# Retention, MoE and SOLU on one core: one two-bank PSUM tile for each attention unit, a fixed order of its products, and state products on 64x64 quarters

## The chip, the cores and the metric

One Trainium2 chip, one of its cores. The metric is the device time of one execution, in microseconds; of a kernel's runs the median counts. TensorE multiplies into PSUM, which has eight banks of 128 x 512 float32; VectorE and ScalarE read PSUM and write SBUF; GpSimd helps from SBUF; SyncE issues most of the DMA transfers.

## The reference

Three stages in a row. The first is a retention (linear attention with a decaying state), for 4 batches, 8 heads, 768 tokens and a head size of 64; the second a feed-forward with a piecewise activation; the third a feed-forward with a softmax-gated activation and a normalisation.

```python
gamma = 1.0 - 2.0 ** (-5.0 - np.arange(H))
for t in range(S):
    state = gamma * state + einsum('bhd,bhe->bhde', k[:, :, t], v[:, :, t])
    y[:, :, t] = scale * einsum('bhd,bhde->bhe', q[:, :, t], state)
x = y.transpose(0, 2, 1, 3).reshape(3072, 512)
...
h = x @ w_in                                   # 512 -> 2048
g = where(h >= 1, h, where(h <= -1, 0, (h + 1) ** 2 / 4))
x = g @ w_out                                  # 2048 -> 512
...
h = x @ w2_in                                  # 512 -> 1024
solu = h * softmax(h)
ln = (solu - mean) / sqrt(var + 1e-6) * g_ln
out = ln @ w2_out                              # 1024 -> 512
```

## The kernel before

**Attention.** The 768 tokens of a batch are six chunks of 128. A unit `u` is one chunk of one batch with all eight heads; there are 24, `u = 6 * batch + chunk`. Heads go in four pairs `p`; in `qk` (transposed, head size on the partitions) the first head of a pair (`o = 0`) lies on partitions 0 to 63 and the second (`o = 1`) on 64 to 127. A unit has two groups of products, all in float32, where one product becomes two matrix instructions:

- the first products, L153: `k` by `q` within the chunk, eight products, `o = 0` into PSUM tile `qp0` and `o = 1` into `qp1`, each with the 64 rows of its half of the array. VectorE multiplies each tile by a decay mask (`sm`, L162).
- the second group: queries by the state (L173, four products on the whole array; the state is block diagonal in a pair, so half of what is multiplied is zero), masked scores by values (L177, eight products, each into 64 output partitions) into `pv`, and the update of the state (L183, eight products of 64 columns) into `sp`. A unit that is first in its batch (0, 6, 12, 18) has no L173, one that is last (5, 11, 17, 23) no L183.

Then `split` (L88, L89) writes `pv` as a rounded part `xh` and a rest `xl` into the x tiles of its block, and ScalarE and VectorE scale the state and add `sp` to it (L190, L196).

**MoE.** Tokens are also cut into six blocks of 512, four units each (units 0 to 3 make block 0, and so on). A slot is one block and one of 16 slices `f` of the 2048 columns: `moe_h` does 12 products of 512 columns (L273) into `hp`, ScalarE and VectorE make `gh` and `gl` from it, and `moe_out` does 12 more (L301) into four accumulators two slots later. The order of the slots is written out in `segs`: block 0 with f 0 to 5, block 1 with f 0 to 11, block 0 with f 6 to 15, block 1 with f 12 to 15, then blocks 2 to 5 whole. The x tiles are double buffered by block, so those of block 2 take the place of block 0's. The weights arrive as 64-bit words and are converted on ScalarE and VectorE (`conv_w`), slice by slice ahead of their first use, up to some 155 us.

**SOLU.** From about 640 us on, 24 token tiles go through `h2` (L400), transposes (L441) and `outp` (L452).

**What sets the order.** The program's text gives priorities, and a planner with its own model of times puts the instructions of each engine in an order; the engines then run that order and wait where data isn't there. Attention from unit 8 on is traced with a raised priority (`HP_ATT`), so that the planner takes its instructions as soon as it thinks them ready.

**PSUM.** `ps_acc` has four banks (the accumulators, units 0 to 3, parts of SOLU), `ps_h` two, and `ps_a` two tiles of one bank each. From unit 4 on a unit's four tiles take turns in `ps_a`: `qp0`, `qp1`, `pv`, `sp`. A tile can be written when the one before it in that bank has been read.

Of the kernel before, what the change touches and what calls it, by code (L numbers as in the profile page):

```python
# [9 lines left out]
F32 = mybir.dt.float32  # L10
# [4 lines left out]
ALU = mybir.AluOpType  # L15
# [20 lines left out]
NWP = 2 * CPB  # L36
STEP0 = 7
W0 = -4
# [10 lines left out]
def kernel(  # L49
# [24 lines left out]
    ps_a = ctx.enter_context(tc.tile_pool(name="ps_a", bufs=2, space=bass.MemoryType.PSUM))  # L74
# [6 lines left out]
    gdec = const.tile([128, NPAIR, 1], F32, tag="gdec", name="gdec")  # L81
    g_sb = const.tile([128, NF2], F32, tag="g_sb", name="g_sb")

    def fl(t):
        return t.bitcast(F32)

# [42 lines left out]

    def attention(u, env):  # L130
# [4 lines left out]
        ppool, ptag = (ps_acc, "acc") if blk == 0 else (ps_a, "pa")  # L135
        early = u < NWP

# [6 lines left out]
        with (ExitStack() if early else tc.issue_after(state["last_w"].ins)):  # L144
            nc.sync.dma_start(qk, qk_t[b, c])
            nc.sync.dma_start(kv, kv_t[b, c])
        yield
        yield
        qp = [ppool.tile([128, NPAIR, C], F32, tag=ptag, name=f"qp{o}") for o in range(2)]
        for p in range(NPAIR):  # L150
            for o in range(2):
                r = slice(64 * o, 64 * o + 64)
                pe.matmul(qp[o][:, p, :], qk[r, 1, p, :], qk[r, 0, p, :], start=True, stop=True)  # L153
        if not first:
            qn = attp.tile([128, NPAIR, C], F32, tag="qn", name="qn", bufs=1)
            ve.tensor_tensor(out=qn, in0=qk[:, 0], in1=qdec, op=ALU.mult)
# [3 lines left out]
        for o in range(2):  # L160
            t = attp.tile([128, NPAIR, C], F32, tag="sm", name="sm", bufs=2)
            ve.tensor_tensor(out=t, in0=qp[o], in1=dmat[:, o], op=ALU.mult)  # L162
# [7 lines left out]
        pv = ppool.tile([128, NPAIR, C], F32, tag=ptag, name="pv")  # L170
        if not first:
            for p in range(NPAIR):
                pe.matmul(pv[:, p, :], st[:, p, :], qn[:, p, :],  # L173
                          start=(p == 0), stop=False, skip_group_check=True)
        for p in range(NPAIR):
            for o in range(2):
                pe.matmul(pv[64 * o:64 * o + 64, p, :], kv[:, 1, 2 * p + o, :], sm[o][:, p, :],  # L177
                          start=(first and p == 0), stop=(p == NPAIR - 1), skip_group_check=True)
        if not last:
            sp = ppool.tile([128, NPAIR, D], F32, tag=ptag, name="sp")  # L180
# [353 lines left out]
```

## Time and profile before

| | us |
|---|---|
| three runs | 931.03, 931.36, 934.76 |
| median | 931.36 |
| profiled execution | 931.8 |
| its span (first to last instruction) | 930.1 |
| TensorE busy in the span | 918.8 |
| VectorE, ScalarE, GpSimd busy | 579.4, 396.4, 26.3 |

The busy time of an engine is the time in which it had at least one instruction running; matrix instructions are pipelined, so their lengths overlap, and what a group costs is read from its start to the start of the next one. The rest of the profiled time lies outside the span. The TensorE clock that was granted is 1.00 in most stretches and lower in two windows of the first 17 us.

### The profile page before, as it was taken

To read this page: it belongs to the slowest core of one execution; us is meant where nothing else is said; L and a number is where in the kernel's file an instruction comes from. 1 tells how busy PE (TensorE), PEld (TensorE's weight loads), DVE (VectorE), ACT (ScalarE), POOL (GpSimd) and SP (SyncE) were. 2 spreads that over 40 slices of the span, in tenths; PEclk is the share of its full clock that TensorE was granted. 3 is DMA by queue.
4 is the path that set the end of the run, shared out by engine and by line. 5 is a ranking of instruction groups with operands and counts; after the bars stand their busy time and mean duration, and the time that the engine had idled before them with its cause. 6 is when DMAs were issued, how large, how long until landed. Compare 5 with 4: busy or idle time off the path is not lost.

```text
span 930.1 us, 12709 instructions
## 1 busy us (share of the span) xinstructions
PE 918.8 (99%) x4936; PEld 758.8 (82%) x4936; DVE 579.4 (62%) x1332; ACT 396.4 (43%) x725; POOL 26.3 (3%) x28
## 2 busy tenths in 40 slices
PE   8899999999999999999999999999999999999998
PEld 7788888887888887888888888888888888888886
DVE  5999997234444324422336238932988888888884
ACT  2668866333233333333336338842333333333322
POOL 3100100000010000000000000000000000000000
PEclk8999999999999999999999999999999999999999
DMA  9921821005342203200024004211101010100000
GB/s 344 417 111 46 314 72 46 24 1 163 122 123 69 68 23 113 69 23 1 23 85 165 1 0 159 76 64 46 45 35 69 24 69 23 69 23 24 24 24 35
DMA packets 25004, 75.08 MB, mean 81 GB/s; under 512 B 3184, under 2 KB 3312, under 8 KB 24176
## 3 DMA queue, kind: packets, MB, share of 16 engines
q1 hardware_dynamic: 23792, 72.18, 21.6%
q10 hardware_dynamic: 1152, 2.10, 0.9%
q8 instruction: 39, 0.64, 0.3%
q14 instruction: 21, 0.17, 0.1%
HBM read 59.58 MB, written 14.68 MB: 80 GB/s over the span
## 4 chain that ended last, share of the span: by engine, by line
PE 94%; DMA 4%; DVE 1%; ACT 1%; SPq 0%; issue 0%; DVEq 0%; ACTq 0%
PE acc L301 28%; PE hp L273 28%; PE h2p L400 14%; PE op L452 14%; PE qp L153 3%; PE tp L441 2%; PE pv L177 2%; PE pv L173 2%; DMA w_raw<-in_w_in_dram 1%; DMA xs<-x2p 1%; DMA kv<-in_kv_t_dram 1%; PE sp L183 1%; DMA dmat<-in_xtab_dram 0%; DVE xs L314 0%; DVE wm L111 0%
## 5 line engine op out<-in xcount | busy, mean ns | idle before, releaser
L301 PE MATMUL acc<-gh,w 128*128 128x512 f32 x768 | 198.6, 391 | 0.4 <-DVE xs L314 0.4
L273 PE MATMUL hp<-xh,w 128*128 128x512 f32 x768 | 195.1, 392 | 1.5 <-ACT w L116 0.8
L273 PEld LDWEIGHTS hp<-xh,w 128*128 128x128 f32 x768 | 143.0, 188 | 32.7 <-ACT xh L88 0.9
L301 PEld LDWEIGHTS acc<-gh,w 128*128 128x128 f32 x768 | 143.4, 188 | 31.5 <-DVE xs L314 1.0
L281 DVE SCALAR_TENSOR_TENSOR cs<-cs,hp 128x512 f32<-128x512 f32 x96 | 65.8, 685 | 149.4 <-ACT cs L280 149.0
L279 ACT ACTIVATE cs<-hp,half 128x512 f32<-128x512 f32 x96 | 66.1, 689 | 206.5 <-PE hp L273 193.1
L301 PE MATMUL acc<-gl,w 128*128 128x512 f32 x384 | 110.8, 393 | 0.0
L273 PE MATMUL hp<-xl,w 128*128 128x512 f32 x384 | 106.2, 393 | 0.0
L400 PE MATMUL h2p<-w,x2h 128*128 128x512 f32 x384 | 97.1, 395 | 0.0
L89 DVE TENSOR_TENSOR gl<-cs,gh 128x512 fp32r<-128x512 f32 x96 | 67.8, 706 | 40.5 <-ACT gh L88 40.1
L452 PE MATMUL op<-w,lh 128*128 128x512 f32 x384 | 91.4, 390 | 0.2 <-ACT lh L88 0.2
L273 PEld LDWEIGHTS hp<-xl,w 128*128 128x128 f32 x384 | 71.5, 188 | 15.9 <-issue 0.3
L452 PEld LDWEIGHTS op<-w,lh 128*128 128x128 f32 x384 | 71.9, 188 | 15.4 <-ACT lh L88 0.5
L301 PEld LDWEIGHTS acc<-gl,w 128*128 128x128 f32 x384 | 71.5, 188 | 15.6 <-issue 0.3
L88 ACT ACTIVATE gh<-cs 128x512 fp32r<-128x512 f32 x96 | 60.5, 630 | 51.1 <-DVE cs L281 50.7
L400 PEld LDWEIGHTS h2p<-w,x2h 128*128 128x128 f32 x384 | 70.5, 188 | 13.7
L280 ACT ACTIVATE cs<-cs 128x512 f32<-128x512 f32 x96 | 60.6, 631 | 2.7 <-ACT cs L279 0.2
L410 ACT ACTIVATE e<-h2p,st 128x512 f32<-128x512 f32 x48 | 32.6, 686 | 50.1 <-DVE st L427 38.3
L400 PE MATMUL h2p<-w,x2l 128*128 128x512 f32 x192 | 51.6, 390 | 0.0
L162 DVE TENSOR_TENSOR sm<-qp,dmat 128x512 f32<-128x512 f32 x48 | 31.8, 685 | 27.8 <-PE qp L153 26.4
L88 ACT ACTIVATE x2h<-x2r 128x512 fp32r<-128x512 f32 x24 | 15.1, 631 | 77.8 <-PE h2p L400 59.5
L452 PE MATMUL op<-w,ll 128*128 128x512 f32 x192 | 47.7, 390 | 0.0
(66 smaller groups left out, 1013.1 us busy)
## 6 DMA issues: line engine op xcount, KB each, us to landing
qk<-in_qk_t_dram SPq DMA_DIRECT2D x24, 512.0 KB, 4.3
kv<-in_kv_t_dram SPq DMA_DIRECT2D x24, 512.0 KB, 4.1
w_raw<-in_w_in_dram SPq DMA_DIRECT2D x24, 512.0 KB, 8.0
w_raw<-in_w_out_dram SPq DMA_DIRECT2D x24, 512.0 KB, 6.8
x2d<-xs SPq DMA_DIRECT2D x24, 256.0 KB, 2.7
x2r<-x2d SPq DMA_DIRECT2D x6, 1024.0 KB, 4.8
out_dram<-o SPq DMA_DIRECT2D x24, 256.0 KB, 2.0
x2p<-xs SPq DMA_DIRECT2D x8, 256.0 KB, 2.7
```

The lines of the kernel that those rows point to most:

```text
L88: sc.activation(hi, src, AF.Copy)
L89: ve.tensor_tensor(out=lo, in0=src, in1=fl(hi), op=ALU.subtract)
L153: pe.matmul(qp[o][:, p, :], qk[r, 1, p, :], qk[r, 0, p, :], start=True, stop=True)
L162: ve.tensor_tensor(out=t, in0=qp[o], in1=dmat[:, o], op=ALU.mult)
L273: pe.matmul(hp, l[:, k * 128:(k + 1) * 128], r[:, k, :], start=(n == 0), stop=(n == 3 * KD - 1))
L279: sc.activation(cs, hp, AF.Relu, bias=half, scale=0.5)
L280: sc.activation(cs, cs, AF.Square)
L281: ve.scalar_tensor_tensor(cs, cs, 1.0, hp, op0=ALU.min, op1=ALU.max)
L301: pe.matmul(acc[d][:, :BLK], l[:, d * 128:(d + 1) * 128], r, start=(first and m == 1), stop=(last and m == 3))
L400: pe.matmul(hps[n], l[:, k, :], w2i[k, n][part], start=(m == 0), stop=(m == 3 * KD - 1))
L410: sc.activation(e[:, n, :], hps[n], AF.Exp, bias=st[:, 2:3], accum_out=st[:, 3 + n:4 + n])
L452: pe.matmul(op, l[:, f, :], w2o[f][part], start=(n == 0), stop=(n == 3 * NF2 - 1))
```

## The change

- `ps_a` holds one tile of two banks (`pa`). From unit 4 on a unit takes it once for `qp0` and `qp1`, and writes `pv` and `sp` into the same tile afterwards; the next unit takes it when everything of this one has been read. In `h2` every other token tile uses it too.
- `in_row` ties the TensorE instructions traced inside it to the order in which they are traced, each to the one before, with an edge for the planner and no wait on the chip. From unit 4 on it holds the first products, and the second group, of a unit.
- From unit 12 on (`quad`) pairs 2 and 3 are loaded with their two heads exchanged between the partition halves (`load_swapped`: three transfers in place of one). The state of a head is kept in 64 x 64, and the product with it reads one half of the rows and writes one half of the output partitions: eight products, two for each of the four quarters. `pv` is two tiles, one a bank, by the half of the rows that was read; `sp` shares the second bank. `split` goes in four pieces of 64 partitions. Unit 12 also makes exchanged copies of the decay tables.

```diff
@@ -1,4 +1,4 @@
-from contextlib import ExitStack
+from contextlib import ExitStack, contextmanager
 import numpy as np
@@ -34,7 +34,9 @@
 SA, SB = 6, 12
 LD, CL = 7, 4
 NWP = 2 * CPB
+QUAD = 2 * NCH
 STEP0 = 7
+ROW = CPB
 W0 = -4
 WARM = 40
 PER = 4
@@ -71,7 +73,7 @@
     cv = ctx.enter_context(tc.tile_pool(name="cv", bufs=2))
     ps_acc = ctx.enter_context(tc.tile_pool(name="ps_acc", bufs=4, space=bass.MemoryType.PSUM))
     ps_h = ctx.enter_context(tc.tile_pool(name="ps_h", bufs=2, space=bass.MemoryType.PSUM))
-    ps_a = ctx.enter_context(tc.tile_pool(name="ps_a", bufs=2, space=bass.MemoryType.PSUM))
+    ps_a = ctx.enter_context(tc.tile_pool(name="ps_a", bufs=1, space=bass.MemoryType.PSUM))
     x2d = [dpool.tile([128, KD, BLK], F32, tag=f"x2d{b}", name=f"x2d{b}") for b in range(NBLK)]
     x2p = [dpool.tile([128, KD, BLK], F32, tag=f"x2p{b}", name=f"x2p{b}") for b in range(2)]
@@ -79,10 +81,24 @@
     half = const.tile([128, 1], F32, tag="half", name="half")
     vdec = const.tile([128, H, 1], F32, tag="vdec", name="vdec")
     gdec = const.tile([128, NPAIR, 1], F32, tag="gdec", name="gdec")
+    gdec2 = const.tile([128, NPAIR, 1], F32, tag="gdec2", name="gdec2")
     g_sb = const.tile([128, NF2], F32, tag="g_sb", name="g_sb")
     def fl(t):
         return t.bitcast(F32)
+    @contextmanager
+    def in_row():
+        done, last = {i.name for i in nc.cur_bb.bb.instructions}, None
+        yield
+        for i in nc.cur_bb.bb.instructions:
+            if i.name in done or i.engine != mybir.EngineType.PE:
+                continue
+            if last is not None:
+                tc.add_manual_dep(i, last.name, mybir.DependencyInfo(
+                    mybir.DependencyClass.NoSync, mybir.DependencyReason.DATA), reason="in a row")
+            last = i
     def split(src, hi, lo):
         sc.activation(hi, src, AF.Copy)
@@ -127,13 +143,34 @@
+    def load_swapped(dst, src):
+        n = NPAIR // 2
+        ax = (slice(None),) * (len(dst.shape) - 3)
+        nc.sync.dma_start(dst[(slice(None), *ax, slice(0, n))], src[(slice(None), *ax, slice(0, n))])
+        for h in range(2):
+            nc.sync.dma_start(dst[(slice(64 * h, 64 * h + 64), *ax, slice(n, 2 * n))],
+                              src[(slice(64 - 64 * h, 128 - 64 * h), *ax, slice(n, 2 * n))])
     def attention(u, env):
         b, c = divmod(u, NCH)
         first, last = c == 0, c == NCH - 1
         blk, cb = divmod(u, CPB)
         attp = env["attp"]
-        ppool, ptag = (ps_acc, "acc") if blk == 0 else (ps_a, "pa")
-        early = u < NWP
+        if blk == 0:
+            def banks(*names):
+                return [ps_acc.tile([128, 512], F32, tag="acc", name=n) for n in names]
+        else:
+            both = []
+            def banks(*names):
+                if not both:
+                    both.append(ps_a.tile([128, 2, 512], F32, tag="pa", name="pa"))
+                return [both[0][:, n] for n in range(len(names))]
+        early, quad = u < NWP, u >= QUAD
         def tile_of(name, *shape):
             if early:
@@ -142,24 +179,40 @@
         qk, kv = tile_of("qk", NPAIR, C), tile_of("kv", H, D)
         with (ExitStack() if early else tc.issue_after(state["last_w"].ins)):
-            nc.sync.dma_start(qk, qk_t[b, c])
+            if not quad:
+                nc.sync.dma_start(qk, qk_t[b, c])
+            else:
+                load_swapped(qk, qk_t[b, c])
             nc.sync.dma_start(kv, kv_t[b, c])
         yield
         yield
-        qp = [ppool.tile([128, NPAIR, C], F32, tag=ptag, name=f"qp{o}") for o in range(2)]
-        for p in range(NPAIR):
-            for o in range(2):
-                r = slice(64 * o, 64 * o + 64)
-                pe.matmul(qp[o][:, p, :], qk[r, 1, p, :], qk[r, 0, p, :], start=True, stop=True)
+        if u == QUAD:
+            env["qdec"] = cv.tile([128, NPAIR, C], F32, tag="wp", name="qdec2", bufs=2)
+            env["gdec"] = gdec2
+            with tc.issue_after(state["last_w"].ins):
+                load_swapped(env["qdec"], xtab_d)
+                load_swapped(gdec2, gdec_d)
+            gp.tensor_tensor(out=env["qdec"], in0=env["qdec"], in1=gdec2.to_broadcast([128, NPAIR, C]), op=ALU.mult)
+            env["dmat"] = [cv.tile([128, NPAIR, C], F32, tag="wm", name="dmat2", bufs=3) for _ in range(2)]
+            for r in range(2):
+                sc.activation(env["dmat"][r][:, :2], dmat[:, r, :2], AF.Copy)
+                sc.activation(env["dmat"][r][:, 2:], dmat[:, 1 - r, 2:], AF.Copy)
+        qp = [t.rearrange("a (p c) -> a p c", p=NPAIR) for t in banks("qp0", "qp1")]
+        with (in_row() if u >= ROW else ExitStack()):
+            for p in range(NPAIR):
+                for o in range(2):
+                    r = slice(64 * o, 64 * o + 64)
+                    pe.matmul(qp[o][:, p, :], qk[r, 1, p, :], qk[r, 0, p, :], start=True, stop=True)
         if not first:
             qn = attp.tile([128, NPAIR, C], F32, tag="qn", name="qn", bufs=1)
-            ve.tensor_tensor(out=qn, in0=qk[:, 0], in1=qdec, op=ALU.mult)
+            ve.tensor_tensor(out=qn, in0=qk[:, 0], in1=env["qdec"], op=ALU.mult)
         if not last:
             gp.tensor_tensor(out=kv[:, 0], in0=kv[:, 0], in1=vdec.to_broadcast([128, H, D]), op=ALU.mult)
         sm = []
         for o in range(2):
             t = attp.tile([128, NPAIR, C], F32, tag="sm", name="sm", bufs=2)
-            ve.tensor_tensor(out=t, in0=qp[o], in1=dmat[:, o], op=ALU.mult)
+            ve.tensor_tensor(out=t, in0=qp[o], in1=env["dmat"][o], op=ALU.mult)
             sm.append(t)
         yield
         if cb == 0:
@@ -167,21 +220,58 @@
                              env["xp"].tile([128, KD, BLK], F32R, tag="xl", name="xl"))
         xh, xl = env["x"][blk]
         tk = slice(cb * C, cb * C + C)
-        pv = ppool.tile([128, NPAIR, C], F32, tag=ptag, name="pv")
-        if not first:
-            for p in range(NPAIR):
-                pe.matmul(pv[:, p, :], st[:, p, :], qn[:, p, :],
-                          start=(p == 0), stop=False, skip_group_check=True)
-        for p in range(NPAIR):
-            for o in range(2):
-                pe.matmul(pv[64 * o:64 * o + 64, p, :], kv[:, 1, 2 * p + o, :], sm[o][:, p, :],
-                          start=(first and p == 0), stop=(p == NPAIR - 1), skip_group_check=True)
-        if not last:
-            sp = ppool.tile([128, NPAIR, D], F32, tag=ptag, name="sp")
+        if quad:
+            res = banks("pv0", "pv1")
+            pv = [t[:, :256].rearrange("a (j c) -> a j c", j=2) for t in res]
+            sp = res[1][:, 256:].rearrange("a (p d) -> a p d", p=NPAIR)
+            with (in_row() if u >= ROW else ExitStack()):
+                if not first:
+                    for j in range(2):
+                        for g in range(2):
+                            for r in range(2):
+                                o = r ^ g
+                                pe.matmul(pv[r][64 * o:64 * o + 64, j, :], st[64 * r:64 * r + 64, 2 * g + j, :D],
+                                          qn[64 * r:64 * r + 64, 2 * g + j, :], start=(j == 0), stop=False, skip_group_check=True)
+                for r in (1, 0):
+                    for j in range(2):
+                        for o in range(2):
+                            p = 2 * (r ^ o) + j
+                            pe.matmul(pv[r][64 * o:64 * o + 64, j, :], kv[:, 1, 2 * p + o, :], sm[r][:, p, :],
+                                      start=(first and j == 0), stop=(j == 1), skip_group_check=True)
+                if not last:
+                    for p in range(NPAIR):
+                        for r in range(2):
+                            h = 2 * p + (r ^ (p // 2))
+                            pe.matmul(sp[64 * r:64 * r + 64, p, :], kv[:, 0, h, :], kv[:, 1, h, :],
+                                      start=True, stop=True, skip_group_check=True)
+            for r in (1, 0):
+                for o in range(2):
+                    g, rows = r ^ o, slice(64 * o, 64 * o + 64)
+                    split(pv[r][rows], xh[rows, 2 * g:2 * g + 2, tk], xl[rows, 2 * g:2 * g + 2, tk])
+            if first:
+                ve.tensor_copy(st[:, :, :D], sp)
+            elif not last:
+                for p in range(NPAIR):
+                    sc.activation(st[:, p, :D], st[:, p, :D], AF.Copy, scale=gdec2[:, p, :])
+                ve.tensor_tensor(out=st[:, :, :D], in0=sp, in1=st[:, :, :D], op=ALU.add)
+            return
+        res = banks("pv", "sp")
+        pv = res[0].rearrange("a (p c) -> a p c", p=NPAIR)
+        sp = res[1][:, :NPAIR * D].rearrange("a (p d) -> a p d", p=NPAIR)
+        with (in_row() if u >= ROW else ExitStack()):
+            if not first:
+                for p in range(NPAIR):
+                    pe.matmul(pv[:, p, :], st[:, p, :], qn[:, p, :],
+                              start=(p == 0), stop=False, skip_group_check=True)
             for p in range(NPAIR):
                 for o in range(2):
-                    pe.matmul(sp[64 * o:64 * o + 64, p, :], kv[:, 0, 2 * p + o, :], kv[:, 1, 2 * p + o, :],
-                              start=True, stop=True)
+                    pe.matmul(pv[64 * o:64 * o + 64, p, :], kv[:, 1, 2 * p + o, :], sm[o][:, p, :],
+                              start=(first and p == 0), stop=(p == NPAIR - 1), skip_group_check=True)
+            if not last:
+                for p in range(NPAIR):
+                    for o in range(2):
+                        pe.matmul(sp[64 * o:64 * o + 64, p, :], kv[:, 0, 2 * p + o, :], kv[:, 1, 2 * p + o, :],
+                                  start=True, stop=True)
         split(pv, xh[:, :, tk], xl[:, :, tk])
         if last:
             return
@@ -220,7 +310,7 @@
     st = attp.tile([128, NPAIR, 128], F32, tag="state", name="state", bufs=1)
     gp.memset(st, 0.0)
-    env = {"attp": attp, "xp": xp, "x": {}}
+    env = {"attp": attp, "xp": xp, "x": {}, "qdec": qdec, "gdec": gdec, "dmat": [dmat[:, o] for o in range(2)]}
@@ -391,8 +481,11 @@
         def h2(t):
             hi, lo = x2s.pop(t)
-            pool, tag = ((ps_a, "pa"), (ps_acc, "acc"))[t % 2]
-            hps = [pool.tile([128, 512], F32, tag=tag, name="h2p") for _ in range(2)]
+            if t % 2:
+                hps = [ps_acc.tile([128, 512], F32, tag="acc", name="h2p") for _ in range(2)]
+            else:
+                pa = ps_a.tile([128, 2, 512], F32, tag="pa", name="h2p")
+                hps = [pa[:, n] for n in range(2)]
             for n in range(2):
                 m = 0
                 for (l, part) in ((hi, 0), (hi, 1), (lo, 0)):
```

## Rows read from the trace of the kernel before

**Rows 1.** Part 1 of the page: busy time, share of the span, instructions of each engine.

```profile
PE 918.8 (99%) x4936; PEld 758.8 (82%) x4936; DVE 579.4 (62%) x1332; ACT 396.4 (43%) x725; POOL 26.3 (3%) x28
```

**Rows 2.** Timeline of TensorE (start, length, group, count), unit 14 and unit 15's first products.

```profile
271.69 1.16 PE L153 MATMUL qp<-qk 64*128 64x128 f32 x16
272.78 1.43 PE L301 MATMUL acc<-gh,w 128*128 128x512 f32 x5
274.04 1.07 PE L301 MATMUL acc<-gl,w 128*128 128x512 f32 x4
274.95 1.98 PE L273 MATMUL hp<-xh,w 128*128 128x512 f32 x8
...
277.90 1.05 PE L173 MATMUL pv<-qn,state 128*128 128x128 f32 x8
278.88 1.09 PE L177 MATMUL pv<-sm,kv 128*64 128x128 f32 x16
279.81 0.63 PE L183 MATMUL sp<-kv 128*64 128x64 f32 x16
280.37 1.89 PE L301 MATMUL acc<-gh,w 128*128 128x512 f32 x7
...
285.83 1.16 PE L153 MATMUL qp<-qk 64*128 64x128 f32 x16
```

**Rows 3.** Timeline of TensorE, the first half of unit 17's first products.

```profile
312.68 1.98 PE L273 MATMUL hp<-xh,w 128*128 128x512 f32 x8
314.59 1.16 PE L153 MATMUL qp<-qk 64*128 64x128 f32 x8
315.67 1.19 PE L273 MATMUL hp<-xl,w 128*128 128x512 f32 x4
```

**Rows 4.** Timeline of TensorE, unit 18, its second group of products.

```profile
358.99 0.43 PE L177 MATMUL pv<-sm,kv 128*64 128x128 f32 x2
359.36 0.49 PE L273 MATMUL hp<-xl,w 128*128 128x512 f32 x1
359.78 0.98 PE L177 MATMUL pv<-sm,kv 128*64 128x128 f32 x13
...
361.26 0.73 PE L273 MATMUL hp<-xl,w 128*128 128x512 f32 x2
```

**Rows 5.** Windows of all engines: length, busy us of each, then granted clock, DMA.

```profile
10.00:17.00 7.00, 7.00 (x74) 6.20 (x72) 4.65 (x8) 1.87 (x5) 2.92 (x3) 0.61 1.02 390
...
40.00:77.00 37.00, 37.00 (x244) 29.86 (x244) 35.39 (x66) 23.65 (x43) 1.04 (x1) 1.00 0.35 143
...
245.00:345.00 100.00, 99.98 (x635) 81.97 (x634) 39.27 (x63) 35.41 (x65) 5.76 (x5) 1.00 0.27 85
```

**Rows 6.** Timeline of TensorE, first gap of unit 0 (in brackets: idle before).

```profile
9.78 0.48 PE L177 MATMUL pv<-sm,kv 128*64 128x128 f32 x1 [3.22 <-DVE sm L162]
```

**Rows 7.** Timeline of VectorE, the weight conversion that block 0's f=5 waits for.

```profile
72.18 0.68 DVE L117 TENSOR_TENSOR w<-wm,w 128x512 fp32r<-128x512 f32 x1
```

**Rows 8.** Timeline of TensorE, h of block 0, f=5.

```profile
74.02 2.01 PE L273 MATMUL hp<-xh,w 128*128 128x512 f32 x8
```

**Rows 9.** Timeline of ScalarE, units 8 and 9 leave PSUM.

```profile
201.74 1.09 ACT L88 ACTIVATE xh<-pv 128x512 fp32r<-128x512 f32 x2 [1.79 <-PE hp L273]
```

**Rows 10.** Timeline of TensorE, units 9, 10, 11 and the first h of block 2.

```profile
207.75 0.69 PE L183 MATMUL sp<-kv 128*64 128x64 f32 x16
208.37 1.16 PE L153 MATMUL qp<-qk 64*128 64x128 f32 x8
...
227.97 1.16 PE L153 MATMUL qp<-qk 64*128 64x128 f32 x16
...
241.74 1.07 PE L273 MATMUL hp<-xh,w 128*128 128x512 f32 x4
```

**Rows 11.** Timeline of all engines, unit 14 on VectorE and ScalarE.

```profile
273.10 1.28 DVE L162 TENSOR_TENSOR sm<-qp,dmat 128x512 f32<-128x512 f32 x2
...
281.45 0.69 DVE L89 TENSOR_TENSOR xl<-pv,xh 128x512 fp32r<-128x512 f32 x1
```

## The prediction

> **What bounds the kernel now.** I read the page's busy times first: TensorE is busy for 918.8 of 930.1 us and no other engine for more than 62% [rows 1]. So only TensorE time that goes away, or a new TensorE wait, can move the end. Next the windows: between 245 and 345 us TensorE stands for 0.02 us of 100, with VectorE and ScalarE at some 40% [rows 5]. Then the timeline of TensorE, to see what a unit of attention costs there and what it costs its neighbours. Last, two places where another engine paces the work: the start, where VectorE is full (35.39 of 37 us [rows 5]), and the step into block 2.
>
> The reader should see three things in the timeline. Sixteen first products in a row, which alternate between the two row halves, take 1.09 us (271.69 to 272.78, [rows 2]); eight of one half alone take 1.08 us too (314.59 to 315.67, [rows 3]). So the halves run side by side if they alternate, and a unit whose two banks are filled in two separate groups pays 2.17. I count eight such units among the twenty from unit 4 on: 5, 6, 9, 10, 12, 17, 21 and 22. Second, a group costs its neighbours something: eight MoE products take 1.91 us before it instead of 1.81, five take 1.26 behind it instead of 1.13 (at 0.227 each, from 274.04 to 274.95) [rows 2, 3]. That is 0.10 in and 0.13 out. Third, in units 6, 10, 12, 18 and 22 the second group is torn apart, as the second `sm` comes after the first product.
>
> **The change, part by part.** The sum is made against the profiled execution's 931.8 us, 0.4 above the median of 931.36; it carries over to the median unchanged.
>
> One tile and a fixed order for the first products. The two banks come free together, so the planner has no reason to start one half early: 8 x 1.09 = 8.7 us saved [rows 3]. Each of these units also loses one cut, 0.2 x 8 = 1.6.
>
> The fixed order of the second group. Torn, `pv` and `sp` take 0.37 + 1.48 = 1.85 us and the single MoE product between them 0.42 instead of 0.23 [rows 4]; whole they take 0.93 + 0.56 = 1.49 [rows 2]. That is 0.55 a unit. Unit 6 starts with `pv` and may still be torn; units 12, 18 and 22 now begin with bank 1, which needs the later `sm`, and unit 10's `sm` are no longer apart. 4 x 0.55 = 2.2. Smaller bits (two units in part side by side, late `sp` groups) I leave out; they would add below 1 us.
>
> Products with the state on quarters, ten units (13 to 17, 19 to 23). Now eight instructions on the whole array take 0.98 us [rows 2]. Afterwards there are sixteen, four in each quarter. The trace has no quarter, so I bound it. If all four quarters run at once at the pace of the column halves of `pv` (16 in 0.93, so 0.116 a pair [rows 2]), four rounds take 0.46. If only two run at once, sixteen take 0.93. Between them, `sp` shows sixteen loads and products in 0.56 [rows 2], the fastest pace of such pairs shown; I take 0.56, on the assumption that quarters are issued no faster than that row shows. The way in now costs 0.10, since the group no longer opens in the MoE's own mode [rows 3]. Saved: 0.98 - 0.56 - 0.10 = 0.32 a unit, 3.2 in all; ends of the range 0.42 and -0.05 a unit, +4.2 and -0.5.
>
> A rule speaks against this edit: the Trainium skill, "TensorEngine Tiling (Array Packing)", section Tiling Modes, says that changing the tiling mode drains the engine, and a quarter group adds a change of mode. The trace agrees in that MoE products beside a group of another mode lose 0.10 and 0.13 [rows 2, 3], which the sum above has counted. The page "TensorE: Matmul & The Clock Gate", Part 3, gives some 4 ns for each further tile that runs beside the first; worked out from it, an estimate, four rounds of 0.116 with three such steps each would take about 0.51, and the end would come 0.5 us earlier.
>
> What I cost at nothing. In the quarter units `pv` leaves PSUM in four pieces instead of one on ScalarE and VectorE; were each piece as dear as the whole (0.69 on VectorE [rows 11]), that is 2.1 us more a unit, on engines that are 60% idle there [rows 5]. The new tables of unit 12 (two loads with halves exchanged, one product on GpSimd, four copies on ScalarE) and the two further loads a unit on SyncE lie in the same stretch; the buffers they use are those of the weight conversion, which is over. If that cover were gone, a unit would come 2 us later, and only its deadline would matter; a block runs its 16 slots meanwhile. The two-bank `h2p` tile in the last part takes the banks it took before, every other token tile.
>
> Two places give some of it back. First the start. The last conversion that block 0's f=5 needs ends at 72.86 [rows 7], its h starts at 74.02 [rows 8], and VectorE is full from 40 to 77 [rows 5]. Products saved before that let TensorE arrive earlier at weights that aren't there. Units 5 and 6 bring 2 x 1.29 = 2.6 of the sum; I keep 0.5, so -2.1. At best all is kept; at worst the one tile also delays unit 7 and 2 us more go.
>
> Second, the step into block 2. The x tiles of block 2 come free when block 0's last h is done: at 201.74 units 8 and 9 leave PSUM together [rows 9]. Both could wait there, one bank each, with their own work done. With one tile unit 8 holds both banks until then, so unit 9's first products wait at the tile, and units 9, 10 and 11 all have to follow before the first h of block 2, which now starts at 241.74 [rows 10]; that h and everything behind it on TensorE wait for unit 11. On SyncE's queue the `kv` load of unit 11 waits for unit 9's `sp`, with block 0's stores behind it, which are due later still. What TensorE has to do meanwhile: of the 40.0 us some 11.3 are attention (one late `sp`, unit 10, unit 11, half of unit 12, priced as above), so 28.7 are MoE; with three whole units (3 x 3.92 less one `sp`, 11.2) it has 39.9. The chain at the planner's pace is 6.0 to the first product (201.74 to 207.75), two units of 14.1 (271.69 to 285.83) and 10.5 from a unit's first product to the end of its `xl` [rows 2, 9 to 11]: 44.7, so 5 us of it have nothing beside them. In these TensorE really stands only for the other engines' work: `sm` ends 1.6 us behind the products (274.38, [rows 11]), and `xh` takes 0.55 [rows 9] and some 0.35 to be seen. I take -2.5; ends 0 and the rival below. In all 8.7 + 1.6 + 2.2 + 3.2 - 2.1 - 2.5 = 11.1, so 920.3.
>
> **The rivals.** *The wait at the tile is the larger term (slower).* Place: units 9 to 11. Unit 10 took 19.6 us to unit 11 (208.37 to 227.97, [rows 10]). At that pace for all three the chain is 6.0 + 2 x 19.6, and 16.0 for the last (10.5 and the same 5.5 more), 61.2, and TensorE stands 21 us: 931.4 - 13.6 + 21 = 939. It decides from a stand of 13.6 us (no gain), or 18.3 (slower by 0.5%). For it: nothing else is left to run there, and after a gap of 3.22 us the granted clock was 0.61 over the next 7 [rows 5, 6]. Against it: unit 10's 19.6 came with its two halves apart, which the change ends.
>
> *The quarters don't run four at a time.* The term is -0.5 instead of +3.2: 924. For it: no row shows more than two at once.
>
> *Nothing is given back.* The planner finds other work at the start and the step into block 2 is covered: 11.1 + 2.1 + 2.5 = 15.7, so 915.7.
>
> *The change doesn't do what it says.* The order binds a unit's products to each other, and not against others between them. If MoE products slip in, the pairs break and the first two parts bring nothing: 931.4 - 3.2 + 2.5 = 930.7. Against it: where both halves were ready, the planner put sixteen in a row [rows 2].
>
> **How the numbers follow.** Forecast 0.52, quarters two at a time 0.15, nothing given back 0.15, no pairs 0.10, long wait 0.08. The likeliest alone reaches from 916 to 924 (the ends of the quarters' term, and 2 either way at the start). The range leaves out the long wait and the broken pairs, 0.18: down to 913 (nothing given back, quarters at 0.46 and the small bits), up to 927 (quarters two at a time and 3 us more of standing). 0.5%, some 4.7 us, is about what a measurement of this kernel can tell from no change. Faster by more (below 926.7): 0.52 + 0.15 + 0.15 = 0.82; within it 0.10; slower 0.08.
>
> **What would show it.** Sixteen first products in 1.09 us in every unit from 4 on; second groups whole; the state's sixteen in about 0.56 in units 13 to 17 and 19 to 23. No gain up to 77 us. A gap of 1 to 3 us on TensorE ahead of block 2's first h, with `sm` or `xh` as its releaser, and unit 9's first products right behind unit 8's `xl`. It would be wrong if gaps of more than 10 us stood there or fell at the granted clock 0.5, if the state's group took 0.9, or if such gaps came back at each later block.

## The result, and the profile after

The changed kernel takes 922.03 us in the median (921.52 to 922.83, four runs) against 931.91 of the kernel before in the same runs; the ratio is 0.9891 (95% interval 0.9871 to 0.9911). That is 9.9 us less; 11.1 were forecast. Its profiled execution has a span of 919.7 us.

Part 1 of its page, which answers to [rows 1]:

```profile
PE 902.7 (98%) x5016; PEld 742.3 (81%) x5016; DVE 581.2 (63%) x1358; ACT 406.2 (44%) x765; POOL 29.0 (3%) x29
```

TensorE is busy for 16.1 us less and stands for 5.7 us more (span less busy: 17.0 instead of 11.3). The forecast had 15.7 us of work going away, so that side of it came out; a third came back as waiting.

The timeline of TensorE in unit 14, which answers to [rows 2] (L206 are the first products, L233 the quarters, L239 and L245 the values and the state's update):

```profile
278.69 1.16 PE L206 MATMUL pa<-qk 64*128 64x128 f32 x16
279.78 0.73 PE L363 MATMUL hp<-xl,w 128*128 128x512 f32 x2
...
285.91 0.67 PE L233 MATMUL pa<-qn,state 64*64 64x128 f32 x16
286.50 1.09 PE L239 MATMUL pa<-sm,kv 128*64 128x128 f32 x16
287.43 0.63 PE L245 MATMUL pa<-kv 128*64 128x64 f32 x16
287.99 2.11 PE L391 MATMUL acc<-gh,w 128*128 128x512 f32 x8
```

The first products take 1.09 us as before. The state's sixteen on quarters take 0.59 (285.91 to 286.50), against 0.98 on the whole array.

What TensorE waited for (total, times, longest), the four longest rows without those of units 0 to 3 and of the warm-up; one of the two waits for `xh` is that of the first h of block 0, at 27.75 us:

```profile
PE pa L264 <- DVE sm L215: 3.1, 2, 1.6
PE acc L391 <- DVE xs L404: 2.4, 2, 1.3
PE hp L363 <- ACT xh L104: 1.4, 2, 0.7
PE acc L391 <- ACT gh L104: 1.3, 1, 1.3
```

And the gaps themselves, in the timeline of TensorE (in brackets, before the group):

```profile
33.73 1.16 PE L264 MATMUL pa<-qn,state 128*128 128x128 f32 x8 [1.63 <-DVE sm L215]
37.67 1.20 PE L363 MATMUL hp<-xh,w 128*128 128x512 f32 x4 [0.17 <-DVE w L133]
45.15 2.11 PE L391 MATMUL acc<-gh,w 128*128 128x512 f32 x8 [1.34 <-ACT gh L104]
...
221.65 0.96 PE L391 MATMUL acc<-gh,w 128*128 128x512 f32 x3 [1.29 <-DVE xs L404]
237.81 1.13 PE L264 MATMUL pa<-qn,state 128*128 128x128 f32 x8 [1.48 <-DVE sm L215]
240.66 3.92 PE L363 MATMUL hp<-xh,w 128*128 128x512 f32 x16 [0.70 <-ACT xh L104]
257.36 0.73 PE L391 MATMUL acc<-gh,w 128*128 128x512 f32 x2 [1.14 <-DVE xs L404]
```

Here the reader sees two places: units 4 and 5 at the start, and the step from block 0 over block 1's end into block 2. The two gaps behind `xs` (the tile into which the partial sums of a block are loaded back) were not in the forecast. The kernel before had three gaps in these two places:

```profile
34.32 1.16 PE L173 MATMUL pv<-qn,state 128*128 128x128 f32 x8 [1.02 <-DVE sm L162]
37.73 1.20 PE L273 MATMUL hp<-xh,w 128*128 128x512 f32 x4 [0.77 <-ACT w L116]
...
229.50 0.73 PE L301 MATMUL acc<-gh,w 128*128 128x512 f32 x2 [0.37 <-DVE xs L314]
```

To compare kernels I add up, from the first h of block 0 to the end, what each of the four kinds of attention product takes for units 4 to 23 (each piece of TensorE's timeline from its start to the next one's, less the gap ahead of that), and the gaps up to 520 us. What is left is MoE, SOLU, the cost of changing between kinds and the gaps at the end. The start is left out: TensorE has the same 256 products there in every kernel, but the first h came at 28.95 us in the profiled execution before and at 27.75 in the one after (last section). So 1.2 of the 10.4 us between the two spans lie ahead of it.

| kernel | from first h | first products | with state | values + update | gaps | left |
|---|---|---|---|---|---|---|
| before | 901.2 | 31.4 | 17.1 | 30.3 | 2.2 | 820.2 |
| order alone | 896.0 | 25.4 | 16.8 | 28.9 | 4.8 | 820.2 |
| quarters alone | 895.9 | 28.3 | 13.1 | 29.1 | 5.1 | 820.3 |
| two-bank tile alone | 895.0 | 22.0 | 17.8 | 29.4 | 6.0 | 819.8 |
| order and quarters | 903.6 | 27.7 | 16.1 | 28.7 | 6.0 | 825.1 |
| tile and order | 897.0 | 22.0 | 16.9 | 28.1 | 9.1 | 820.9 |
| tile and quarters | 892.9 | 21.9 | 13.1 | 28.1 | 8.7 | 821.2 |
| changed (all three) | 892.0 | 22.1 | 13.0 | 28.1 | 7.8 | 821.0 |

In the row of the two-bank tile alone, unit 4 ran at a granted clock of 0.50 (last section), which is in its 17.8 and 29.4.

### The profile page after: what moved, and what is told of

Its sections match the earlier page's. It is cut to its first block, busy times and chain, and to the rows that moved or that the text cites. A ratio compares the mean times of both kernels' runs of the same rounds, so it can differ in the third digit from the quotient of the medians.

```text
span 919.7 us, 12967 instructions
## 1 busy us (share of the span) xinstructions
PE 902.7 (98%) x5016; PEld 742.3 (81%) x5016; DVE 581.2 (63%) x1358; ACT 406.2 (44%) x765; POOL 29.0 (3%) x29
## 4 chain that ended last, share of the span: by engine, by line
PE 93%; DVE 2%; DMA 2%; ACT 1%; issue 0%; SPq 0%; ACTq 0%; DVEq 0%
PE acc L391 28%; PE hp L363 27%; PE h2p L493 14%; PE op L545 14%; PE tp L534 2%; PE pa L206 2%; PE pa L239 1%; DMA xs<-x2p 1%; PE pa L268 1%; PE pa L233 1%; PE qp L206 1%; PE pv L268 1%; PE pa L264 1%; DMA x2d<-xs 0%; PE pa L245 0%
## 5 line engine op out<-in xcount | busy, mean ns | idle before, releaser
L363 PE MATMUL hp<-xl,w 128*128 128x512 f32 x384 | 103.2, 390 | 0.0
L500 DVE TENSOR_REDUCE st<-h2p 128x1 f32<-128x512 f32 x48 | 32.0, 688 | 18.4 <-PE h2p L493 18.3
```

The lines of the kernel that those rows point to most:

```text
L363: pe.matmul(hp, l[:, k * 128:(k + 1) * 128], r[:, k, :], start=(n == 0), stop=(n == 3 * KD - 1))
L500: ve.tensor_reduce(st[:, n:n + 1], hps[n], axis=AX.X, op=ALU.max)
```

## The experiments

All were timed in five rounds; ratios are to the kernel before, with their 95% intervals.

**Which of the three parts does what.** The first four undo one or two parts.

Order and quarters without the tile (`two_tiles`):

```diff
-ps_a = ... tile_pool(name="ps_a", bufs=1, ...)
+ps_a = ... tile_pool(name="ps_a", bufs=2, ...)
...
-                if not both:
-                    both.append(ps_a.tile([128, 2, 512], F32, tag="pa", name="pa"))
-                return [both[0][:, n] for n in range(len(names))]
+                return [ps_a.tile([128, 512], F32, tag="pa", name=n) for n in names]
...
-                pa = ps_a.tile([128, 2, 512], F32, tag="pa", name="h2p")
-                hps = [pa[:, n] for n in range(2)]
+                hps = [ps_a.tile([128, 512], F32, tag="pa", name="h2p") for _ in range(2)]
```

Expected: 

> Order and quarters stay, the two-bank tile goes back to two tiles of one bank. If the fixed order makes the pairs (my theory): sixteen first products in 1.09 us in every unit from 4 on as in the changed kernel, and since the second product of a unit has to wait for the second bank, unit 9 is held up to block 0's last h as well: 920.5 to 923.5 us, with the gaps of 1 to 2 us before block 2's first h still there. Rival (the one tile holds unit 9 back): unit 9 runs early again, those gaps go, 918 to 920.5 us. Rival (the one tile makes the pairs): half of the units fall apart, 927 us or more.

Measured: 933.28 us, 1.0021 (1.0012 to 1.0030): no gain is left, and my theory fell. The timeline of TensorE in this kernel, units 13 and 14 (L204 first products, L231 quarters):

```profile
257.77 0.48 PE L204 MATMUL qp<-qk 64*128 64x128 f32 x2
258.18 0.50 PE L389 MATMUL acc<-gl,w 128*128 128x512 f32 x1
258.62 1.16 PE L204 MATMUL qp<-qk 64*128 64x128 f32 x14
...
280.35 0.43 PE L231 MATMUL pv<-qn,state 64*64 64x128 f32 x2
280.71 0.50 PE L361 MATMUL hp<-xh,w 128*128 128x512 f32 x1
281.14 0.66 PE L231 MATMUL pv<-qn,state 64*64 64x128 f32 x14
281.73 1.09 PE L237 MATMUL pv<-sm,kv 128*64 128x128 f32 x16
```

The first product's two instructions go alone (0.41 us to the start of what follows), MoE comes in, and then the other fourteen take 1.09 like sixteen; so it is in 14 of the 20 units. The quarters are torn in the same way in nine of ten units (0.36 and 0.59). The order keeps the sequence and leaves room between. That the first bank comes free earlier, and the planner uses it, is my reading of this; no run shows the planner's reason. What is left also rises by 4.9 us, as each torn group is cut in and out once more: TensorE changes between attention and MoE 126 times from the first h on, 96 times in the kernel before, so some 0.33 us for each of the 15 groups more.

The tile alone (`tile_only`: `ROW = NU`, `QUAD = NU`).

Expected: 

> The two-bank tile alone, without the order and the quarters. If the fixed order makes the pairs: some units still come apart as before, and the held-back unit 9 stays, so 928 to 932 us. Rival (two banks that come free together are enough for the planner): sixteen in a row in at least 18 of 20 units, and only the quarters' 0.3 us in ten units are missing, 924 to 926 us.

Measured: 925.07 us, 0.9944 (0.9926 to 0.9963). All twenty units have sixteen in a row with no order given: the rival was right. Its eight runs spread from 922.95 to 930.46 us, more than those of the changed kernel.

Tile and quarters without the order (`no_order`):

```diff
-ROW = CPB
+ROW = NU
```

Expected: 

> The changed kernel without the fixed order; tile and quarters stay. If the fixed order makes the pairs, in the first products and in the quarters: the four quarters are taken in another order, the state's group takes 0.6 to 1.0 us, and pairs break: 925 to 930 us. Rival (the tile is enough): 921 to 923 us, rows as in the changed kernel.

Measured: 921.18 us, 0.9895 (0.9882 to 0.9908), the same as the changed kernel. The rows are whole and the quarters take 0.60 without it. Beside the tile, the fixed order does nothing that can be measured.

Tile and order without the quarters (`no_quad`):

```diff
-QUAD = 2 * NCH
+QUAD = NU
```

Expected: 

> The changed kernel with the state's products on the whole array in all units. Changed kernel: ten groups of 0.60 us; before: 0.98 with no cost at the way in, about 0.09 at the way in now. So 10 x 0.29 = 2.9 us slower than the changed kernel, 924 to 926 us. Rival (what the quarters save is lost to four-piece readout and the added mode change): within 1 us of the changed kernel, 921 to 923 us.

Measured: 926.37 us, 0.9948 (0.9929 to 0.9966). In the table the products with the state are 3.9 us dearer than in the changed kernel (16.9 against 13.0). The profiled executions differ by 5.0 us from the first h on; the rest is 1.3 us more of gaps, with 4.0 us of wait for `xs` instead of 2.4. The runs spread from 923.56 to 929.55 us, so the 4.3 us between the medians can't be shared out more closely.

The quarters alone (`quads_only`: as `two_tiles`, and `ROW = NU`).

Expected: 

> The quarters alone: two tiles of one bank, no fixed order. If the two-bank tile makes the pairs and the fixed order costs where the banks come free apart: TensorE's pairs fall apart as in the kernel before, but it doesn't pay the order's torn groups (0.41 + 1.09 for the first products, 0.36 + 0.59 for the state's), so it lies between: 926 to 930 us, 3 to 7 us faster than with the order. Rival (the tile's absence and not the order makes the loss of the version with two tiles): 932 to 934 us as that one.

Measured: 926.86 us, 0.9956 (0.9940 to 0.9972). The quarters keep their 4.0 us (13.1 against 17.1), and without the order they are never torn. The first products gain 3.1 us as well (28.3 against 31.4): from unit 13 on all units have sixteen in a row, also 17 and 21, which fell apart before, while 5, 6, 9, 10 and 12 fall apart still. So the one tile is not the only way to whole groups.

The order alone (`order_only`: as `two_tiles`, and `QUAD = NU`).

Expected: 

> The fixed order alone: two tiles of one bank, state on the whole array. If the order costs where the banks come free apart (first products torn 2 and 14: 0.41 + 1.09 us instead of 1.09, or 2.17 as two halves): 932 to 938 us, no faster than the kernel before. Rival (the order makes pairs by itself): 925 us or less.

Measured: 926.98 us, 0.9950 (0.9937 to 0.9962). Neither was right: the order alone does help, as 2 and 14 (1.50, in eight units) are less than 8 and 8 (2.17), and in twelve units the sixteen stay whole. It harms only together with the quarters: there more units are torn, and the quarters themselves. That their first product then also waits on one bank of two is my reading. Alone, the order, the quarters and the tile bring some 5, 5 and 6 us; these don't add up to the 9.9 of all three, as each makes some of the same groups whole. Its trace also shows that the hold at block 2 is not the tile's alone. Unit 9 on TensorE's timeline:

```profile
128.32 0.49 PE L204 MATMUL qp<-qk 64*128 64x128 f32 x2
...
202.63 1.16 PE L204 MATMUL qp<-qk 64*128 64x128 f32 x14
```

Its first product runs at 128 us and the other fourteen wait 74 us for unit 8's bank, until block 0's last h.

**The step into block 2.** `late_8` puts eight slots of block 1 behind block 0 instead of four:

```diff
-SA, SB = 6, 12
+SA, SB = 6, 8
```

Expected: 

> The changed kernel with block 1 left after f 7 instead of f 11, so that eight slots of block 1 lie between block 0's last h and block 2's first, instead of four. If units 9, 10 and 11, which one tile holds back until block 0's last h, have too little MoE work beside them (44.7 us of chain against 39.9 of work): four slots are 21.8 us more, the gaps of 1.48 (sm) and 0.70 (xh) go, 2 us faster, 919.5 to 920.5 us. Rival (the planner's order leaves such gaps wherever the units lie): gaps stay, 922 us. Rival (f 8 to 15 are needed 20 us earlier and the conversion isn't ready): TensorE waits for weights near 110 to 180 us, 923 us or more.

Measured: 919.83 us, 0.9873 (0.9860 to 0.9885), 2.2 us faster than the changed kernel. What TensorE waited for in it (the rows that matter here):

```profile
PE pa L264 <- DVE sm L215: 1.7, 1, 1.7
PE hp L363 <- DVE cs L371: 1.2, 3, 0.8
PE acc L391 <- DVE xs L404: 1.2, 1, 1.2
PE hp L363 <- ACT xh L104: 0.7, 1, 0.7
```

The `sm` wait has one occurrence left, that of the start, and the `xh` wait only that of the first h: both gaps at block 2 are gone, and one of the two behind `xs`. Three short waits for `cs` (1.2 us) are new.

**The gaps behind the partial sums.** On ScalarE's queue of the changed kernel:

```profile
213.39 4.16 ACTq L403 DMA_DIRECT2D xs<-x2p  x2
219.26 0.69 ACT L369 ACTIVATE cs<-hp,half 128x512 f32<-128x512 f32 x1 [6.25 <-DMA x2d<-xs]
```

Two loads of partial sums into `xs` take 4.16 us to issue, and the readout of the next h behind them waits on ScalarE for 6.25, by the profile until a store out of `xs` has landed: the buffer has to be stored before it can be loaded. The kernel before had the same hold, shorter:

```profile
223.42 1.97 ACTq L313 DMA_DIRECT2D xs<-x2p  x2
226.56 0.69 ACT L279 ACTIVATE cs<-hp,half 128x512 f32<-128x512 f32 x1 [4.21 <-DMA x2d<-xs]
```

`xs_apart` gives the sums the buffers of the weight conversion:

```diff
-                xs = moe.tile([128, BLK], F32, tag="cs", name="xs", bufs=3)
+                if fresh or (blk and d > 1):
+                    xs = moe.tile([128, BLK], F32, tag="cs", name="xs", bufs=3)
+                else:
+                    xs = cv.tile([128, BLK], F32, tag=("wm", "wp")[d % 2], name="xs", bufs=(3, 2)[d % 2])
```

Expected: 

> The changed kernel, but the partial sums of blocks 0 and 1 are read back into the buffers of the weight conversion, which is over, instead of the three that MoE's own tiles use. If TensorE's gaps of 1.29 and 1.14 us behind the sums (221.65 and 257.36) come from the wait for a buffer (its store has to land before the next load is issued, and ScalarE's queue stands behind that load): both gaps go, 2.0 to 2.5 us faster than the changed kernel, 919 to 920.5 us. Rival (the transfers themselves are too slow): gaps stay, 921.5 to 922.5 us.

Measured: 919.17 us, 0.9863 (0.9850 to 0.9876), 2.9 us faster. In its waits (the rows that matter here) no `xs` is left:

```profile
PE pa L264 <- DVE sm L215: 3.2, 2, 1.7
PE hp L363 <- ACT xh L104: 1.4, 2, 0.7
PE acc L391 <- ACT gh L104: 0.9, 1, 0.9
```

The two `xs` waits were 2.43 us; the wait for `gh` at the start is 0.47 shorter too, which goes with something else (last section).

`both` joins the two edits. Expected: 

> Both of these in one kernel. If the two waits are separate: 4.2 to 4.6 us faster than the changed kernel, 917 to 918 us. Rival (one covers the other): 919 to 920 us.

Measured: 918.42 us, 0.9857 (0.9844 to 0.9869): 3.6 us of the 5.1 that the two bring singly, between the two expectations. They share one gap: `late_8` had already removed one of the `xs` waits.

**The start.** `no_clamp` leaves out one VectorE operation of each weight conversion, the clamp at L123.

Expected: 

> The changed kernel with one VectorE operation of each weight conversion left out, the clamp to the smallest and largest float16-like bounds (L123), so that a conversion has four VectorE operations instead of five and values beyond the bounds would come out wrong. If VectorE, full of conversions, sets the pace from 28 to 77 us and gives back what TensorE saves there: its work falls by 0.33 us a conversion, about 4 us by 77 us, TensorE's gaps there (3.1 us: sm 1.63, gh 1.34, w 0.17) fall to 1 us or less and the kernel is 1.5 to 2.5 us faster, 919 to 920.5 us. Rival (the gaps come from the planner's order or from a transfer): they stay, 921.5 to 922.5 us.

Measured: 931.75 us, 0.9995 (0.9986 to 1.0004), 10 us slower than the changed kernel with less work to do. Unit 7 and block 1's first h on its TensorE timeline:

```profile
73.69 1.16 PE L205 MATMUL pa<-qk 64*128 64x128 f32 x16
76.67 2.11 PE L390 MATMUL acc<-gh,w 128*128 128x512 f32 x8 [1.81 <-ACT gh L104]
...
85.28 5.53 PE L362 MATMUL hp<-xh,w 128*128 128x512 f32 x16 [2.82 <-ACT xh L104]
```

Units 5 to 7 come later in it: unit 7's first products start at 73.69 instead of 64.87, and block 1's first h waits for their `xh`. Up to 520 us the gaps add up to 13.5 us instead of 7.8, and the granted clock was 0.68 from 36 to 40 us, where it was 1.00 in the changed kernel. So less work for VectorE changed the order (by the planner's model of shorter conversions, as I take it) and not only the load, and the experiment doesn't tell whether the load was the cause.

`prio_4` gives attention its raised priority from unit 4 on (`if u >= CPB` in `att_slot`). Expected: 

> The changed kernel with the raised priority of attention from unit 4 on instead of unit 8. If the planner's order among conversions and attention, and not VectorE's total work, sets the gaps between 28 and 77 us: units 4 to 7 come earlier, the wait for sm (1.63 us) shrinks and the kernel is 1 to 3 us faster, 919 to 921 us. Rival (the weights are due as early as the attention): TensorE waits for the conversions instead, 922 us or more.

Measured: 922.29 us, 0.9902 (0.9887 to 0.9917): nothing that can be told from the changed kernel, and its gaps at the start are the same three (1.65, 0.17, 1.34). `both_prio` is the same in `both`. Expected: 

> The same priority in the version with separate buffers for the partial sums and eight slots of block 1 behind block 0. If the start and the step into block 2 are separate places: the same gain as in the changed kernel, 916 to 918 us from 918.4. Rival: 918.4 or more.

Measured: 916.98 us, 0.9844 (0.9830 to 0.9857). It beats the kernel before by 14.5 us and the changed one by some 5. Over `both` the intervals overlap, so a gain of the priority is not shown: the gaps of 0.16 and 0.61 for `cs` near 97 and 146 us that `both` still had are gone, and of the start's gaps that for `gh` is 0.86 instead of 1.32, which goes with something else (last section).

## Why the prediction was right, point by point

The time lay in the range and the mechanism of the likeliest case held: the pairs, the quarters four at a time, and some of it given back in two places. That the sum came within 2 us is in part luck: two terms missed by 5.3 us together (cuts and `xs`), and the others came out 3.3 us better than forecast. By terms, from the table and the gaps:

| term | forecast | measured |
|---|---|---|
| first products side by side | -8.7 | -9.3 |
| fewer cuts, singly and beside torn groups | -2.4 | +0.8 |
| torn second groups whole | -1.4 | -2.2 |
| quarters, with the way in | -3.2 | -4.1 |
| gaps at the start | +2.1 | +1.4 |
| gaps of `sm` and `xh` at block 2 | +2.5 | +2.2 |
| gaps behind `xs` | 0 | +2.1 |
| sum | -11.1 | -9.1 |

(The forecast's 1.6 of cuts and 0.2 of each of the four torn groups stand together in the second line. The quarters' way in is measured in the second line and not in the fourth, and the table's sum is the 9.2 from the first h, to its rounding.)

*First products.* Right in size and place. The working gave it to tile and order together. The tile alone is enough for all of it (22.0 in `tile_only`), and beside it the order adds nothing; without the tile the order alone brings 6.0 of the 9.3 and the quarters alone 3.1. The sentence that carried it, that two banks which come free together give the planner no reason to start one half, fits `tile_only`.

*Cuts.* This term was wrong. Each split unit was to lose a cut of 0.2. But in four of the eight a half stood directly against another attention group (the first halves of units 6, 10, 12 and 22 behind the unit before, the second halves of 10 and 22 against their products with the state), so there was no cut to lose: TensorE changes between attention and MoE 96 times before and 80 times after, eight groups fewer for both terms of cuts together. The quarters brought a way in of 0.09 (eight MoE products in 1.90 from 265.85 to 267.75). That is not the whole of the +0.8: tile and order, without quarters, have 820.9 left too. In the changed kernel the MoE products also run slow in places between attention groups of the start (sixteen from 60.64 to 64.87 take 0.6 us more than at 0.227 each, elsewhere 0.24 more); how much each part adds stays open. One second group is still torn, unit 7's (12 and 4 of its products with the values), as the order does not keep MoE out.

*Quarters.* Right: sixteen take 0.59 to 0.60, close to the 0.56 taken and far from the 0.93 of two at a time. The estimate of 0.51 from the Trainium skill, "TensorE: Matmul & The Clock Gate", Part 3, was too low by 0.08. The drain at a change of mode, of which the Trainium skill, "TensorEngine Tiling (Array Packing)", section Tiling Modes, speaks, shows on the way into the quarters as no more than the 0.09.

*Start.* The size was near and the reason not shown. The forecast named weights that aren't there; only 0.17 us of the gaps wait for a weight (0.77 before), the others for `sm` (1.63), which VectorE makes, and `gh` (1.34), which ScalarE makes from `cs` of VectorE. Some 0.5 of the wait for `gh` goes with one long VectorE operation (last section). What else sets these waits stays open: two experiments did not settle it. The sign "no gain up to 77 us" did not quite hold: from the first h to the 200th MoE product, with the same attention done, it is 64.7 us instead of 65.7, so 1.0 us was kept by then, where the forecast kept 0.5 of 2.6.

*Block 2.* Right: 1.48 us for `sm` and 0.70 for `xh` against 1.6 and 0.9, and more MoE work in that place removes both (`late_8`). The working gave the hold to the one tile; with two tiles and the fixed order unit 9 is held as well, so the tile is one way to it.

*What was missed.* The reload of the partial sums, 0.37 us of wait before, shows 2.43 in the changed kernel. The forecast put it at nothing without a word. `xs_apart` shows that the wait is for the buffer and not for the transfer itself, as other buffers remove it. Why it grew is argued only: the hold on ScalarE was there before (4.21 us, then 6.25), and with less work ahead of it TensorE comes to it earlier; but it is 1.7 us with the tile alone and 4.0 with tile and order, so it doesn't simply follow the time saved.

*Rivals.* Quarters two at a time, no pairs and the long wait are excluded by the trace. Nothing given back is excluded too: 5.6 us were.

## What to carry to other kernels

Where halves of the array run side by side only if their instructions alternate (sixteen in 1.09 us here, or 2.17), give them buffers that come free together, and the planner may alternate them by itself, as it did here; a forced order over buffers that come free apart can tear the group and cost more than it brings. Before counting on time taken from the busiest engine, look for the waits of a few tenths already in the trace (a reload, a readout at a block's step): they can be the next bound, as the 0.37 us here that became 2.43. An experiment that takes work away under a planner may also change the order, so compare the orders before reading the time.

## What the hardware showed that I had not expected

Two pieces of one PSUM tile are not read at once in these kernels. In unit 13 of the changed kernel the four pieces of the values alternate between ScalarE and VectorE, each waiting for the other (ScalarE and VectorE, from its timeline):

```profile
269.95 0.38 ACT L104 ACTIVATE xh<-pa 64x256 fp32r<-64x256 f32 x1
270.37 0.42 DVE L105 TENSOR_TENSOR xl<-pa,xh 64x256 fp32r<-64x256 f32 x1 [0.53 <-ACT xh L104]
270.82 0.38 ACT L104 ACTIVATE xh<-pa 64x256 fp32r<-64x256 f32 x1 [0.48 <-DVE xl L105]
...
272.96 0.43 DVE L105 TENSOR_TENSOR xl<-pa,xh 64x256 fp32r<-64x256 f32 x1 [0.45 <-ACT xh L104]
```

The same pieces in `two_tiles`, where each bank is a tile of its own:

```profile
267.25 0.63 ACT L104 ACTIVATE xh<-pv 64x256 fp32r<-64x256 f32 x2
267.64 1.63 DVE L105 TENSOR_TENSOR xl<-pv,xh 64x256 fp32r<-64x256 f32 x4
268.09 0.71 ACT L104 ACTIVATE xh<-pv 64x256 fp32r<-64x256 f32 x2 [0.22 <-DVE xl L105]
```

With one tile it is 3.4 us from the first `xh` to the end of the last `xl`, with two 2.0, and the engines overlap. In both the four pieces lie in two banks and two halves of the partitions, no two in one place; so what takes turns is the tile, not the bank. The profile puts each of these waits down to the other engine's instruction, so the turns lie in the waits of the program; that the memory needs them is not shown. The longer readout is off TensorE's path here.

A VectorE operation that takes 0.68 us in the 47 other places of its line took 1.53 while GpSimd multiplied, which itself took 1.40 instead of its usual 1.04 (start, length):

```profile
41.42 1.40 POOL L211 TENSOR_TENSOR kv<-kv,vdec 128x512 f32<-128x512 f32 x1 [1.96 <-DMA kv<-in_kv_t_dram]
41.84 1.53 DVE L127 SCALAR_TENSOR_TENSOR wm<-w_raw,wm 128x512 uint32<-128x512 uint32 x1
```

It is not always VectorE that loses: at 105.38 us GpSimd's product took 3.09 beside an operation of the same line that took 0.68. At the start it bears on TensorE, as the `cs` from which `gh` is made comes behind this operation on VectorE. Where an operation in that place took 1.53 us (the changed kernel, `prio_4`, `late_8`, `both`) the wait for `gh` is 1.32 to 1.34; where the operation beside GpSimd's took 1.02 (`no_order`) it is 1.07, and where it took about 0.8 (`no_quad`, `xs_apart`, `both_prio`) 0.84 to 0.87. No run was made for it, so the link is read from these eight traces.

A gap of the same size at the start brought the half clock in one execution and not in another. Windows of TensorE (length, busy, granted clock, DMA), the tile alone and then tile and quarters:

```profile
31.00:35.00 4.00, 1.86 (x7) 0.94 1.03 407
35.00:38.00 3.00, 2.94 (x18) 0.50 1.04 414
38.00:41.00 3.00, 3.00 (x29) 0.50 1.02 408
```

```profile
31.00:35.00 4.00, 1.82 (x8) 1.00 1.02 405
35.00:38.00 3.00, 3.00 (x43) 1.00 1.03 412
```

In both TensorE was busy for some 1.8 of the 4 us from 31 on; 0.50 is the lower level, 1.2 GHz, and 1.00 the upper, 2.4. Over all these kernels, which have the same 256 TensorE products ahead of the first h, the granted clock from 10 to 17 us lay between 0.59 and 0.83 and the first h between 29.23 us (at 0.59) and 27.47 (at 0.83). If executions of one kernel differ in the same way, that alone is more than a microsecond between them; no kernel was profiled twice.
